# A hardware loop of two rounds around one wait on VectorE, ahead of the copy of the result

## Chip, cores, metric

One core of a Trainium2 chip. The metric is the device time of one execution in microseconds (us), and the profile is of one execution. PE is TensorE, DVE VectorE, ACT ScalarE, SP the engine that issues the transfers; "q" behind an engine's name means its sequencer, under which the profiles list branches (COMPARE_BRANCH), register arithmetic (ALU_OP, MOVE) and stand-alone waits (EVENT_SEMAPHORE).

## The reference

One token goes through a layer norm, an attention block over the last 4096 keys (32 query heads, 8 key heads) and a gated block of three matrices; the results are added to the token:

```python
x = A_x
xn = _layernorm(x, axis=-1)
return x + _A_ref(xn, A_k_cache, A_v_cache, A_wq, A_wo) + _B_ref(xn, B_w_r, B_w_gate, B_w_up, B_w_down)
```

With one row everything is a vector by a matrix, so the bytes to be loaded (30.7 MB) matter more than the arithmetic: in the profile before, DMA is 76% of the chain that ended last.

## The kernel before

All weights and caches come over one queue on SP. The last matrix, `B_w_down`, comes in four chunks of 7, 4, 2 and 1 rows per partition, each with its own semaphore:

```python
wd_chunks = [(0, 7), (7, 11), (11, 13), (13, 14)]
t_wd = [dma(sy, f"wd{k}", wd_sb[:, j0 * D:j1 * D], wd_v[:, j0 * D:j1 * D]) for k, (j0, j1) in enumerate(wd_chunks)]
# ... cut ...
    DVE.need(t_g4, t_rf)
    fill(2)
    t_part = DVE.mark(ve.tensor_tensor(out=part, in0=a_ps, in1=rf, op=ALU.add))      # L542
    PE.need(t_hT)
    for k, (j0, j1) in enumerate(wd_chunks):
        PE.need(t_wd[k])
        for j in range(j0, j1):
            ins = by_halves(hTr[:, j, 0:1], wd_sb[:, j * D:(j + 1) * D], stop=(j == FB - 1))   # L528
        if k == 0:
            PE.need(t_part, t_sel4)
            by_halves(sel4[:], part)
    t_a = PE.mark(ins)
    DVE.need(t_a)
    ACT.need(t_a)
    t_r0 = DVE.mark(ve.tensor_copy(out=res[:, 0:HD], in_=g_ps[0]))                   # L554
    t_r1 = ACT.mark(ac.copy(out=res[:, HD:], in_=g_ps[1]))                           # L555
    SP.need(t_r0, t_r1)
    t_out = dma(sy, "out", out.rearrange("a b d -> (a b) d"), res)
```

`need` puts a semaphore wait on an engine and `mark` lets an instruction raise that engine's counter. PE multiplies the chunks as they land; when its last product is done, VectorE copies the left half of the result and ScalarE the right half; when both are done, SP sends the output.

## Time and profile before

| | before |
|---|---|
| time, median of 6 runs | 79.82 us (79.73 to 79.94) |
| span of the profile, granted TensorE clock | 77.8 us, 1.0 |
| share of DMA in the chain that ended last | 76% |
| third chunk releases PE / fourth chunk releases PE | 75.21 / 75.53 us |
| the two copies start | 75.84 us |
| output issued | 76.30 us |

The chain is read backwards from the last instruction: at each step, what released it. Here it is transfers until 73.3, then PE on the four chunks, then VectorE's copy and the output. The lines that carry this stand in the prediction.

### The profile page before, as it was taken

To read this page: it belongs to the slowest core of one execution; us is meant where nothing else is said; L and a number is where in the kernel's file an instruction comes from. 1 tells how busy PE (TensorE), PEld (TensorE's weight loads), DVE (VectorE), ACT (ScalarE), POOL (GpSimd) and SP (SyncE) were. 2 spreads that over 40 slices of the span, in tenths; PEclk is the share of its full clock that TensorE was granted. 3 is DMA by queue.
4 is the path that set the end of the run, shared out by engine and by line. 5 is a ranking of instruction groups with operands and counts; after the bars stand their busy time and mean duration, and the time that the engine had idled before them with its cause. 6 is when DMAs were issued, how large, how long until landed. Compare 5 with 4: busy or idle time off the path is not lost.

```text
span 77.8 us, 1639 instructions
## 1 busy us (share of the span) xinstructions
PE 55.1 (71%) x640; PEld 28.9 (37%) x642; DVE 43.6 (56%) x96; ACT 30.3 (39%) x41; POOL 10.2 (13%) x22
## 2 busy tenths in 40 slices
PE   0010596479939979979976866877878891998890
PEld 0010311267618658658652342222223440342330
DVE  2779300389049797696945438898886357000301
ACT  2760102328945895895681070443333320000001
POOL 3950000003101032022049100000000000000000
DMA  6999999999999999999999999999999999999800
GB/s 135 387 405 413 438 425 421 425 446 430 472 438 404 413 421 455 446 421 404 408 438 446 446 396 421 412 446 427 413 457 405 430 455 438 404 396 401 319 29 1
DMA packets 2745, 30.72 MB, mean 395 GB/s; under 512 B 307, under 2 KB 438, under 8 KB 822
## 3 DMA queue, kind: packets, MB, share of 16 engines
q1 hardware_dynamic: 2738, 30.67, 93.8%
q8 instruction: 2, 0.03, 0.2%
q14 instruction: 1, 0.01, 0.0%
q10 hardware_dynamic: 4, 0.00, 0.0%
HBM read 30.67 MB, written 0.00 MB: 394 GB/s over the span
## 4 chain that ended last, share of the span: by engine, by line
DMA 76%; PE 9%; ACT 4%; DVE 3%; SPq 3%; issue 1%
DMA k_sb<-in_B_w_down_dram 52%; DMA k_sb<-in_A_k_cache_dram 25%; PE ps L354 5%; ACT kT L329 4%; PE ps L528 3%; SPq L189 3%; DVE kin L321 2%; PE ps L363 1%; DVE kT L326 1%; DVE kT L554 1%; SPq L84 0%; SPq L95 0%
## 5 line engine op out<-in xcount | busy, mean ns | idle before, releaser
L329 ACT COPY kT<-ps 128x1024 bf16<-128x1024 bf16 x19 | 18.5, 1016 | 8.3 <-PE ps L354 8.3
L354 PE MATMUL ps<-perm_bf,kin 128*128 128x128 bf16 x256 | 17.1, 220 | 2.4 <-DVE kin L321 2.1
L354 PEld LDWEIGHTS ps<-perm_bf,kin 128*128 128x128 bf16 x256 | 14.3, 98 | 6.4 <-issue 3.6
L321 DVE COPY kin<-k_sb 128x2048 bf16<-128x2048 bf16 x16 | 10.9, 686 | 4.4 <-DMA k_sb<-in_A_k_cache_dram 3.6
L326 DVE COPY kT<-ps 128x1024 bf16<-128x1024 bf16 x13 | 9.0, 689 | 2.2 <-PE ps L354 1.8
L449 ACT CAST pvS<-ps 128x512 bf16<-128x512 f32 x8 | 4.7, 586 | 10.0 <-PE ps L455 10.0
L363 PE MATMUL ps<-kT,qAB 128*32 128x512 bf16 x68 | 6.8, 389 | 1.9 <-ACT kT L329 1.9
L185 PE MATMUL ps<-zmov,zst 128*128 128x512 bf16 x31 | 7.7, 380 | 0.2 <-issue 0.2
L314 POOL COPY qAB<-qpad 128x64 bf16<-128x64 bf16 x8 | 3.7, 462 | 30.8 <-PE ps L363 30.8
L429 DVE COPY vin<-v_sb 128x2048 bf16<-128x2048 bf16 x8 | 5.5, 686 | 1.1 <-PE ps L464 1.0
L435 DVE COPY vin<-v_sb 128x2048 bf16<-128x2048 bf16 x8 | 5.5, 684 | 0.0
L555 ACT CAST kT<-ps 1x256 bf16<-1x256 f32 x1 | 0.4, 363 | 12.9 <-PE ps L528 12.9
L464 PE MATMUL ps<-vin,pTcur 128*32 128x512 bf16 x32 | 3.2, 386 | 2.6 <-ACT pvS L449 2.2
L476 PE MATMUL ps<-zmov,zst 128*128 128x512 bf16 x16 | 4.7, 376 | 0.0
L542 DVE TENSOR_TENSOR kT<-ps,kT 128x512 f32<-128x512 f32 x1 | 0.7, 691 | 6.5 <-PE ps L523 6.5
L185 PEld LDWEIGHTS ps<-zmov,zst 128*128 128x128 bf16 x32 | 2.7, 98 | 3.7 <-issue 1.3
L238 PE MATMUL ps<-ident_bf,xn_row 1*128 1x1 bf16 x4 | 0.3, 166 | 5.2 <-DVE xn_row L233 5.2
L299 DVE COPY qpad<-ps 128x16 bf16<-128x16 bf16 x4 | 0.5, 170 | 5.5 <-PE ps L294 5.5
L523 PE MATMUL ps<-k_sb,oT 128*1 128x512 bf16 x32 | 2.1, 378 | 2.0 <-DMA k_sb<-in_A_wo_dram 2.0
L470 PE MATMUL ps<-vin,pTcur 128*32 128x512 bf16 x32 | 3.2, 387 | 0.3 <-DVE vin L435 0.2
L282 PE MATMUL ps<-wq_sb,xnT 128*1 128x512 bf16 x32 | 2.9, 499 | 0.6 <-DMA wq_sb<-in_A_wq_dram 0.6
L363 PEld LDWEIGHTS ps<-kT,qAB 128*32 128x32 bf16 x68 | 1.9, 92 | 3.9 <-DVE kT L326 1.1
(95 smaller groups left out, 52.6 us busy)
## 6 DMA issues: line engine op xcount, KB each, us to landing
v_sb<-in_A_v_cache_dram SPq DMA_DIRECT2D x4, 2048.0 KB, 39.1
k_sb<-in_A_k_cache_dram SPq DMA_DIRECT2D x3, 2048.0 KB, 23.7
wq_sb<-in_A_wq_dram SPq DMA_DIRECT2D x2, 2048.0 KB, 9.4
k_sb<-in_A_wo_dram SPq DMA_DIRECT2D x2, 2048.0 KB, 36.1
k_sb<-in_A_k_cache_dram SPq DMA_DIRECT2D x2, 1024.0 KB, 14.2
wq_sb<-in_B_w_gate_dram SPq DMA_DIRECT2D x1, 1792.0 KB, 43.4
wq_sb<-in_B_w_up_dram SPq DMA_DIRECT2D x1, 1792.0 KB, 47.3
k_sb<-in_B_w_down_dram SPq DMA_DIRECT2D x1, 896.0 KB, 40.1
```

The lines of the kernel that those rows point to most:

```text
L185: te.matmul(ps[:, 7, :], lhsT=zst[:], rhs=zmov[:], start=True, stop=True)
L314: gp.tensor_copy(out=qAB[:], in_=qpad[:, g]).then_inc(s_q, 1)
L321: ve.tensor_copy(out=kin[:, 2 * h:2 * h + 2, :], in_=k_sb[:, g, 2 * h:2 * h + 2, :]).then_inc(s_c[h], 1)
L326: ve.tensor_copy(out=kT[:, b, :], in_=tp[:, b, :]).then_inc(s_ev[b], 1)
L329: ac.copy(out=kT[:, b, :], in_=tp[:, b, :]).then_inc(s_ev[b], 1)
L354: ins = te.transpose(tp[:, b, k * P:(k + 1) * P], kin[:, b, k * P:(k + 1) * P], perm_bf[:])
L363: ins = te.matmul(sc[32 * cq:32 * cq + 32, e, :], lhsT=qAB[:, e, :], rhs=kT[:, b, :].rearrange("d (k h q) -> d h k q", h=2, q=PH)[:, e], s ...
L429: ve.tensor_copy(out=vin[:, 0].rearrange("p (q k) d -> p q (k d)", q=4), in_=v_in[:, :, 0:4 * DH]).then_inc(s_va, 1)
L435: ve.tensor_copy(out=vin[:, 1].rearrange("p (q k) d -> p q (k d)", q=4), in_=v_in[:, :, 4 * DH:]).then_inc(s_vb, 1)
L449: ac.copy(out=pvS[:].rearrange("p t d -> p (t d)"), in_=pv_ps).then_inc(s_pvs, 1)
L464: ins = te.matmul(pv_ps[32 * tl:32 * tl + 32, :], lhsT=pTcur[:, tl].rearrange("p q e r -> p (q e r)"), rhs=vin[:, 0].rearrange("p (q t) d ...
L476: te.matmul(ps[:, 7, :], lhsT=zst[:], rhs=zmov[:], start=True, stop=True)
```

## The change

The intent: VectorE is made to run a loop of two rounds, each with a wait for the third chunk, before its copy. In the profile before, the third chunk releases PE at 75.21 us and the copy starts at 75.84, so the wait is met before the copy could start, and what is added is the loop's own work.

```diff
     t_a = PE.mark(ins)
+    with ve.Fori(0, 2):
+        ve.wait_ge(*t_wd[2])
     DVE.need(t_a)
     ACT.need(t_a)
     t_r0 = DVE.mark(ve.tensor_copy(out=res[:, 0:HD], in_=g_ps[0]))
```

## The prediction

What no trace or run of this case shows is cut from the recorded texts, here and below, and the cuts are marked. The sum below came to 0.635 us; its term for the branch back is cut. The terms that stand come to 0.50 us; with the two figures for that branch that the prediction works out from the trace, 0.09 and 0.27, they give its low case of 0.59 and its high case of 0.77. The factor 1.25 in its terms is an estimate, from the semaphore instruction's 21 ns on VectorE against 17 on ScalarE (1.24): with 1.24 each of them rounds to the same hundredth.

> **What bounds the kernel now.** I read the page's slices first, then the chain that ended last in order of time, then the timeline of the last five microseconds, because the change touches only the last wait of VectorE.
>
> The slices and the chain say that the transfers set the pace until about 73 us:
>
> ```profile
> PE   0010596479939979979976866877878891998890
> DVE  2779300389049797696945438898886357000301
> DMA  6999999999999999999999999999999999999800
> ...
> DMA 76%; PE 9%; ACT 4%; DVE 3%; SPq 3%; issue 1%
> ```
>
> The DMA row stands at 9 in nearly every slice, and DMA is 76% of the chain; VectorE (DVE) is almost idle in the last six slices. The end of the chain in order of time:
>
> ```profile
> 33.21 40.08 DMA k_sb<-in_B_w_down_dram
> 73.29 0.14 issue
> 73.43 2.39 PE ps L528 x32
> 75.82 0.02 issue
> 75.84 0.41 DVE kT L554
> ```
>
> The first chunk of A_w_down lands at 73.29, TensorE (PE) then works through the four chunks until 75.82, and VectorE's copy of the result is the last computing step. So a delay of that copy's start moves the end one for one. The timeline of the tail shows how much room there is:
>
> ```profile
> 75.21 0.09 PEld L528 LDWEIGHTS ps<-k_sb,hTr 128*1 128x1 bf16 x4 [0.28 <-DMA k_sb<-in_B_w_down_dram]
> 75.53 0.08 PEld L528 LDWEIGHTS ps<-k_sb,hTr 128*1 128x1 bf16 x2 [0.23 <-DMA k_sb<-in_B_w_down_dram]
> 75.84 0.36 ACT L555 CAST kT<-ps 1x256 bf16<-1x256 f32 x1 [12.86 <-PE ps L528]
> 75.84 0.41 DVE L554 CAST kT<-ps 1x256 bf16<-1x256 f32 x1 [2.92 <-PE ps L528]
> 76.30 0.32 SPq L189 DMA_DIRECT2D out_dram<-kT  x1
> ```
>
> The x4 row is the third chunk (two rows of weights, two halves each): PE was released by its landing at 75.21. The x2 row is the fourth chunk, at 75.53. The two copies start together at 75.84, ScalarE's ends at 76.20, VectorE's at 76.25, and the output is issued at 76.30. The new wait is on the third chunk, so VectorE can leave its first round at about 75.21 and has to be ready for its copy at 75.84: **the slack is 0.63 us**.
>
> [...] The trace has such instructions, and they differ by engine:
>
> ```profile
> L84 ACTq COMPARE_BRANCH  x1: 33/33/33, 1.1 to 1.1; - x1
> ...
> L84 DVEq COMPARE_BRANCH  x1: 47/47/47, 1.1 to 1.1; - x1
> ...
> L84 PEldq COMPARE_BRANCH  x1: 174/174/174, 1.1 to 1.1; - x1
> ```
>
> That is the branch from the first block to the kernel: 33 ns on ScalarE, 47 on VectorE, 174 on TensorE. [...] The 47 against 33 ns (1.42), and the semaphore instruction's 21 ns on VectorE against 17 on ScalarE (1.24), agree that VectorE's sequencer is slower. TensorE's loops show what one round consists of:
>
> ```profile
> L537 PEldq ALU_OP  x8: 36/36/36, 66.5 to 69.3; - x8
> L537 PEldq COMPARE_BRANCH  x8: 83/215/215, 66.6 to 69.4; - x8
> L537 PEldq MOVE  x1: 35/35/35, 66.4 to 66.4; - x1
> ```
>
> One MOVE sets the counter, each round has one ALU_OP and one COMPARE_BRANCH; a branch taken back is 215 ns and the last, not taken, is 83.
>
> [...] the copy before the change began 0.02 us after PE's last matmul ended. [...]
>
> [...] The page's queues show three fetches by the program:
>
> ```profile
> q8 instruction: 2, 0.03, 0.2%
> q14 instruction: 1, 0.01, 0.0%
> ```
>
> **The change part by part.** Nothing is removed. On VectorE the order of instructions gets an ALU_OP that carries the wait for the third chunk and a COMPARE_BRANCH, run twice, after the addition on L542 and ahead of the copy, plus a MOVE ahead of the loop. TensorE gets one unconditional branch after its last matmul, which releases nothing. Transfers and matmuls stay in order.
>
> - MOVE: runs when the addition of L542 has been dispatched, no later than about 72.9, over two microseconds before the wait ends. Cost on the path 0.
> - Two ALU_OP: 36 ns on PE, times 1.25 for the slower sequencer, 45 ns each: 0.09 us (estimate).
> - Branch taken: PE's 215 less its plain branch of 174 leaves 41 for the comparison; with VectorE's own 47 that would be 0.09 us. PE's 215 times 1.25 would be 0.27. [...]
> - Branch not taken: PE's 83 times 1.25 is 0.10 us.
> - Gaps between sequencer instructions: in the trace's single records of PE's loops the COMPARE_BRANCH begins 97 to 102 ns after its ALU_OP began, so the gap is about 61 to 66 ns; times 1.25 about 0.08. There are three: 0.24 us.
> - From the last sequencer instruction to the copy: on VectorE a semaphore wait of 21 ns began at 49.75 and the copy after it at 49.81. I take 0.07 us.
>
> Sum: 0.09 + [...]0.10 + 0.24 + 0.07 = **0.635 us**, against a slack of 0.63. So the loop ends about when PE does. With the low branch it is 0.59 (hidden by 0.04), with the high one 0.77 (a delay of 0.14). As a check, a whole round of PE's loop with four PE instructions in it takes (69.3 - 66.5) / 7 = 0.40 us, and its last half round (36 + 63 + 83) 0.18; together with 0.07 that is 0.65 us, the same. The share of the first round that lies before the wake is nil, since the first ALU_OP itself waits.
>
> The copy itself keeps its 0.41 us, and ScalarE's copy is not delayed, but the output waits for both. Mean expected delay 0.05 to 0.1 us, on 79.82: **79.9 us**, 0.1% up.
>
> **The rivals.**
> 1. *Fully hidden.* Sequencer work of VectorE is cheaper than I make it (47 ns for a plain branch speaks for it). Time 79.8, within the spread of the runs before (79.75 to 79.89).
> 2. *The loop breaks the fetch of instructions.* If the branch back dropped what was already fetched[...], the sequencer would fetch after 75.3. A transfer of 1 KB, the output's, lands about 1.1 us after its issue instruction in the trace, and the fetch packets themselves took 0.3 to 1.0 us; so 1 to 2 us, less nothing, as the slack is spent: 80.9 to 81.9, and the upper end is over 2%. Against it: none of the TensorE loops shows it (the first branch back of L371 took 223 ns, the later ones 207 to 215)[...]. I give it 5%.
> 3. *The tail moves for another reason.* A fetch of 16 KB[...] began at 74.3 in the trace, among the last transfers; a change in layout could move it and with it the last landings, by a few tenths either way. [...] A gain from it would stay under 0.5 us.
> 4. *VectorE waits longer because it sees the third chunk late.* The same semaphore released PE at 75.21; nothing suggests that VectorE sees it later.
>
> **Range and chances.** The centre is 79.9. From below the time is held by the transfers, unchanged, less a few hundredths of noise: 79.7. From above, the high branch (0.14), the spread of the runs (0.07) and some unknown cost of the loop's start (0.1 to 0.2) give 80.25. Two per cent is 1.6 us; only a fetch or a cost three times my estimate would reach it: 4%. Faster by 2% would need shorter transfers, which nothing touches: 1%.
>
> **What would show it right or wrong.** In the changed profile VectorE should have one MOVE, two ALU_OP and two COMPARE_BRANCH of the new line 552, the first ALU_OP at about 75.2 and the last branch over by about 75.8. The gap from PE's last matmul to VectorE's copy, 0.02 us before, should be 0 to 0.2; ScalarE's copy should keep its place behind PE. A branch on VectorE of over 0.3 us, or a new packet of kind "instruction" near 75 us, would show the second rival. Landings that moved relative to the span's start would show the third. A copy that starts a microsecond or more after PE's last matmul would make the prediction wrong.

## The result

| | before | after |
|---|---|---|
| time, median of 6 runs each | 79.82 us (79.73 to 79.94) | 79.77 us (79.66 to 79.78) |
| ratio | | 0.9989 (95%: 0.9976 to 1.0002) |
| span, clock of the profile | 77.8 us, 1.0 | 77.8 us, 1.0 |

The times are the same.

The new line 552 in the profile after, by its instructions (count, duration in ns as least/median/most, first and last start in us):

```profile
L552 DVEq ALU_OP  x2: 40/46/52, 75.2 to 75.5; - x2
L552 DVEq COMPARE_BRANCH  x2: 50/62/73, 75.3 to 75.6; - x2
L552 DVEq MOVE  x1: 44/44/44, 72.2 to 72.2; - x1
```

The MOVE ran at 72.2, while the addition of L542 was being executed; the first ALU_OP waited until 75.2, when the third chunk landed; the last branch began at 75.6. The tail of the timeline after:

```profile
75.21 0.09 PEld L528 LDWEIGHTS ps<-k_sb,hTr 128*1 128x1 bf16 x4 [0.27 <-DMA k_sb<-in_B_w_down_dram]
75.53 0.08 PEld L528 LDWEIGHTS ps<-k_sb,hTr 128*1 128x1 bf16 x2 [0.23 <-DMA k_sb<-in_B_w_down_dram]
75.85 0.36 ACT L557 CAST kT<-ps 1x256 bf16<-1x256 f32 x1 [13.09 <-PE ps L528]
75.85 0.41 DVE L556 CAST kT<-ps 1x256 bf16<-1x256 f32 x1 [2.94 <-PE ps L528]
```

The rows have not moved, and VectorE's copy still starts with ScalarE's, which has no loop in front of it. That is the test to use in all that follows: **ScalarE's copy marks the moment at which PE's end lets a copy begin; the distance of VectorE's copy from it is what the loop costs.** Here it is 0.00.

In the trace's single records the loop reads: ALU_OP 75.199 (52 ns), branch back 75.290 (73 ns), ALU_OP 75.516 (40 ns), branch not taken 75.592 (50 ns), over at 75.642. In the experiments below, where the loop ends late, the copy began 0.045 to 0.046 us after that, so here it was ready at 75.69 (an estimate: 75.642 + 0.046) and waited 0.16 us more for PE.

### The profile page after: what moved, and what is told of

Read it like the earlier page. It is cut to its first block, busy times and chain, and to the rows that moved or that the text cites. A ratio compares the mean times of both kernels' runs of the same rounds, so it can differ in the third digit from the quotient of the medians.

```text
span 77.8 us, 1644 instructions
## 1 busy us (share of the span) xinstructions
PE 56.0 (72%) x640; PEld 29.0 (37%) x642; DVE 43.5 (56%) x96; ACT 30.4 (39%) x41; POOL 10.1 (13%) x22
## 4 chain that ended last, share of the span: by engine, by line
DMA 76%; PE 9%; ACT 4%; DVE 3%; SPq 3%; issue 1%
DMA k_sb<-in_B_w_down_dram 52%; DMA k_sb<-in_A_k_cache_dram 25%; PE ps L354 5%; ACT kT L329 4%; PE ps L528 3%; SPq L189 3%; DVE kin L321 2%; PE ps L363 1%; DVE kT L326 1%; DVE kT L556 1%; SPq L84 0%; SPq L95 0%
## 5 line engine op out<-in xcount | busy, mean ns | idle before, releaser
L542 DVE TENSOR_TENSOR kT<-ps,kT 128x512 f32<-128x512 f32 x1 | 0.7, 691 | 6.7 <-PE ps L523 6.7
L282 PE MATMUL ps<-wq_sb,xnT 128*1 128x512 bf16 x32 | 3.8, 621 | 0.4 <-DMA wq_sb<-in_A_wq_dram 0.4
```

The lines of the kernel that those rows point to most:

```text
L282: ins = te.matmul(ps[32 * c:32 * c + 1, hf, :], lhsT=xnT[:, kt:kt + 1], rhs=wq_sb[:, kt, (4 * hf + c) * 512:(4 * hf + c + 1) * 512], start ...
```

## The experiments

**Theory:** the loop costs VectorE's sequencer about 0.49 us, from the landing of the third chunk to a copy that could start, and 0.65 us lie between that landing and the copy's start anyway. **Rivals:** A, a loop costs once and its rounds next to nothing; B, the end is set elsewhere, whatever VectorE does; C, such work costs the end wherever it lies; D, a wait for a landing is what costs or saves (the expectation of run 4 uses this letter for another one, that two rounds cost nearly nothing); and the fetch rival of the prediction. All runs gave the reference's result. Each ran beside the kernel before on the same chip. In runs 1 to 9 some executions, of the kernel before too, came at 80.5 to 80.9 us with a mean granted clock of 0.978 (others at that clock came at the usual time; runs 8 and 9 show what one of them was); they widen the intervals to some half or whole per cent. So hundredths of a microsecond are read from profiles only, against the same profile's ScalarE copy, and times are used for the larger effects. Eight of the twelve profiles below have a granted clock of 1.0; where it was lower, the text says so.

### 1 and 2: four rounds, eight rounds

```diff
-    with ve.Fori(0, 2):
+    with ve.Fori(0, 4):        # and 8 in the second run
         ve.wait_ge(*t_wd[2])
```

> Four rounds instead of two, same wait for the third chunk. Theory (sequencer work hidden behind the fourth chunk and PE's tail, 0.317 us a round as in the changed trace, 0.13 for the last half round, some 0.05 to the copy): the loop wakes at 75.20 and the copy can start at 75.20 + 3 x 0.317 + 0.13 + 0.05 = 76.33 instead of 75.85, so +0.48 us, 80.25 us. Rival A (a loop costs a fixed amount once, the rounds are nearly free): at most +0.1 us, 79.9. Rival B (the loop is hidden whatever its length, since the end is set elsewhere, by the landing of the output or the drain): 79.8.

> Eight rounds, same wait. Theory: copy at 75.20 + 7 x 0.317 + 0.13 + 0.05 = 77.60, so +1.75 us, 81.5 us, slope 0.317 us a round against the run with four rounds. Rival A (fixed cost): 79.9. Rival B (end set elsewhere): 79.8. If the branch back has to fetch instructions again, a round costs a microsecond or more and it would be over 85 us.

Four rounds: 80.16 us (79.99 to 80.36), before 79.83, ratio 1.0036 (0.9986 to 1.0085). Eight rounds: 81.20 us (81.01 to 81.71), ratio 1.0165 (1.0108 to 1.0222). The times alone resolve only the second. VectorE's copy in the timeline of the run with four rounds, 0.39 us behind ScalarE's at 75.80:

```profile
76.19 0.41 DVE L556 CAST kT<-ps 1x256 bf16<-1x256 f32 x1 [3.35 <-PE ps L528]
```

With eight rounds (profile at clock 0.97) the chain itself runs through the loop. The columns are start, length, what; "issue" is time in which the engine waited for nothing that the profile shows:

```profile
75.44 0.15 issue
75.60 0.04 DVEq L552
75.64 0.04 issue
75.67 0.06 DVEq L552
...
77.44 0.41 DVE kT L556
```

ScalarE's copy began at 75.93, so the loop cost 1.51 us. One round is 0.04 + 0.04 + 0.06 + 0.15: addition, gap, branch, and 0.15 until the next round's first instruction (rounded; 0.278 in the records). Between four and eight rounds the loss grew by 1.51 - 0.39 = 1.12 us, 0.28 a round. Rivals A and B fall. Both losses are smaller than expected (0.48 and 1.75), mainly because I had taken 0.317 for every round, and only the first takes that (its addition 52 ns, its branch 73); the later ones take 0.28. No round shows a microsecond for a fetch.

### 3: eight rounds, begun at the first chunk

```diff
-    with ve.Fori(0, 2):
-        ve.wait_ge(*t_wd[2])
+    with ve.Fori(0, 8):
+        ve.wait_ge(*t_wd[0])
```

> Eight rounds as well, but the wait is for the first chunk of A_w_down, which lands 1.9 us earlier (73.3). Theory (what counts is when the loop can begin, not how long it is): loop over at 73.32 + 7 x 0.317 + 0.13 = 75.67, copy ready at about 75.72, before PE's end at 75.82, so 79.8 us, as before. Rival C (loop work of VectorE's sequencer costs the end its length, or slows semaphores or the queue, wherever it lies): about as the other run with eight rounds, 81.5 us.

79.84 us (79.77 to 80.6) against 79.83, ratio 1.0019 (0.9961 to 1.0078). The copies in the timeline:

```profile
75.86 0.36 ACT L557 CAST kT<-ps 1x256 bf16<-1x256 f32 x1 [11.20 <-PE ps L528]
75.86 0.41 DVE L556 CAST kT<-ps 1x256 bf16<-1x256 f32 x1 [2.96 <-PE ps L528]
```

The same eight rounds that cost 1.51 us now cost none, as they ran from 73.30 to 75.41. Rival C falls: the length of the loop does not count, only when it is over.

### 4: two rounds, begun at the fourth chunk

```diff
-        ve.wait_ge(*t_wd[2])
+        ve.wait_ge(*t_wd[3])
```

> Two rounds, but the wait is for the fourth and last chunk, which lands 0.32 us after the third. Theory: first ALU_OP at about 75.51, last branch over at 75.51 + 0.317 + 0.13 = 75.96, copy at about 76.01 instead of 75.85, so +0.15 to +0.18 us, 79.95 us: the slack left by the change (0.15 us) is less than the 0.32 between the chunks. Rival B (end set elsewhere) and rival D (the change is harmless because two rounds cost nearly nothing): 79.8 us, copy still within 0.03 us of PE's end.

79.97 us (79.81 to 80.18), ratio 1.0007 (0.9969 to 1.0045): the times do not resolve it. The profile does. ScalarE's copy began at 75.88, VectorE's here:

```profile
76.04 0.41 DVE L556 CAST kT<-ps 1x256 bf16<-1x256 f32 x1 [3.10 <-PE ps L528]
```

That is 0.16 us late, within the 0.15 to 0.18 expected. Two rounds do cost; with the third chunk they fit in, with the fourth, 0.32 us later, they do not.

### 5: the wait without a loop

```diff
-    with ve.Fori(0, 2):
-        ve.wait_ge(*t_wd[2])
+    ve.wait_ge(*t_wd[2])
```

> The wait for the third chunk alone, without a loop, ahead of VectorE's copy. Theory: it is over at 75.20, and the copy needs 0.05 us after it, so it starts with PE's end as before, 79.8 us; the copy begins within 0.03 us of PE's last matmul's end, and the output is issued at 76.30. Rival D (what keeps the change harmless is that the loop replaces a wait that was costly): this run would differ from 79.8.

79.97 us (79.72 to 80.87) against 79.95. The profile missed the expectation of 0.03 us; the end of the chain:

```profile
75.82 0.03 issue
75.85 0.02 DVEq L34
75.87 0.04 issue
75.91 0.41 DVE kT L555
```

The copy started 0.07 us behind ScalarE's (75.84), which the change's loop did not cause. With the plain wait the copy has two semaphores to wait for, and the build moved one to an instruction of the sequencer, the 21 ns on L34. It moved the wait for PE, the late one: PE was done at 75.82, the instruction on L34 ran at 75.85, and the copy began 0.04 us after its end. In the change the wait for the chunk sits on the loop's addition, the copy keeps a single wait, and it began 0.02 us after PE's end (75.83 and 75.85). That the place of the late wait makes the difference is a reading; run 12 tests it.

### 6: the loop with nothing to hide behind

```diff
-        ve.wait_ge(*t_wd[2])
+        ve.wait_ge(*t_a)
```

> The same loop of two rounds, but around the wait for PE's last matmul itself, so that nothing is left to hide it behind. Theory: the whole cost of the loop shows, first ALU_OP at about 75.83, then 0.317 + 0.126 + 0.046 = 0.49 us to the copy at 76.32 instead of 75.85: +0.47 us, 80.3 us. With the sum of my prediction (0.635 us) the copy would start at 76.46 and it would be 80.4. Rival B (end set elsewhere): 79.8.

80.22 us (80.12 to 80.92) against 79.95, ratio 1.0034 (0.9949 to 1.0119); here too only the profile resolves it. The end of the chain shows every term of the loop's price:

```profile
75.82 0.05 DVEq L552
75.87 0.04 issue
75.91 0.07 DVEq L552
75.98 0.15 issue
76.14 0.04 DVEq L552
76.18 0.04 issue
76.21 0.05 DVEq L552
76.26 0.04 issue
76.31 0.41 DVE kT L556
```

From 75.82 to 76.31 it is 0.49 us, the theory's figure and not the 0.635 of the prediction. Against ScalarE's copy (75.82) the loss is the same 0.49.

### 7: eight rounds on ScalarE

```diff
-    with ve.Fori(0, 2):
-        ve.wait_ge(*t_wd[2])
+    with ac.Fori(0, 8):
+        ac.wait_ge(*t_wd[2])
```

> Eight rounds on ScalarE ahead of its own copy, waiting for the third chunk; VectorE without a loop. Theory: rounds cost a sequencer's time, [...]so 0.22 us a round (VectorE's later rounds took 0.278) and 0.25 for the first; ScalarE's copy at about 75.20 + 0.25 + 6 x 0.22 + 0.1 + 0.05 = 76.9 and its end at 77.3, where VectorE's copy ends at 76.26; the output waits for both: +1.0 us, 80.8 us. If the round were set by something the engines share (semaphores, memory), 0.28 us as on VectorE and 81.2. If it is like PE's loop (0.4 us with its four instructions) 82.

81.21 us (81.16 to 81.41), ratio 1.0136 (1.0062 to 1.0210); profile at clock 0.97. VectorE's copy, now without a loop, began at 75.78, and ScalarE's here:

```profile
76.88 0.36 ACT L557 CAST kT<-ps 1x256 bf16<-1x256 f32 x1 [13.65 <-issue]
```

ScalarE's later rounds took 0.228 us in the trace's records (addition to addition), VectorE's 0.278: a ratio of 1.22, near the 1.24 of the semaphore instruction (21 against 17 ns in the profile before). The expected 0.22 a round (an estimate, 0.278 over 1.24) held, so a round is the sequencer's own time. The time of 81.21 is the figure that the expectation gave to its rival, a limit that the engines share (81.2), but it doesn't speak for it: by the ratio it is 1.1 us above the kernel before, and ScalarE's copy began 1.10 us behind VectorE's, where the theory said about 1.0 and rounds of 0.28 would have made it 1.4.

### 8 and 9: a probe of the fetch that failed

The prediction gave 5% to a loop that makes the sequencer fetch instructions. The expectations of runs 8 to 11 take a border of two pages of instructions to lie at slot 256; that was an assumption when they were written, and what run 10 shows there is a step: 0.15 to 0.16 us from one no-operation to the next, against 0.03. To force this border into a loop, I put one into VectorE's idle time before L542 of the kernel before, with its first instruction placed by the build at a chosen slot:

```diff
+    with ve.bass.Fori(0, 3, engines=[mybir.EngineType.DVE], head_slot={mybir.EngineType.DVE: 236}):   # 190 in the control
+        for _ in range(22):
+            ve.nop(nofuse=True)
     DVE.need(t_g4, t_rf)
```

> A probe of the rival that a branch back makes the sequencer fetch instructions. Not the change: the kernel before, with a loop of three rounds of 22 no-operations in VectorE's idle time between 65.7 and 72.2 us, whose head is put at slot 236 of 256 so that its body lies across the border of two pages of instructions. If the two pages stay resident: a branch back costs some 0.25 us as in the change, a round 22 x 0.06 to 0.09 + 0.3 = 1.6 to 2.3 us, no packets of kind instruction other than at the entry, and the loop is over by about 73. If the branch back drops the first page: a gap of 1 to 3 us behind each branch taken, with packets of kind instruction beside it, loop over at 75 to 78, and since the addition of L542 comes after it, the time goes up by 2 to 5 us, to 82 to 85.

> The control of the run with the loop across two pages: the same loop with its head at slot 190, so that it ends at 214 and lies in one page. A branch back costs some 0.2 to 0.25 us, a round 1.6 to 2.3 us, no packets of kind instruction beside it. The loop is over by 71 to 73 us; the addition of L542 is ready at 72.2, so the time is 79.8, or up to 0.8 us more if a no-operation takes 0.09 us.

79.85 us (79.71 to 80.83) and 80.22 us (79.57 to 80.67), against 79.95. The traces show why nothing can be read from them: the 22 no-operations are missing, the build had dropped them, so a round was an addition and a branch (slots 236 and 237, by counting) and slot 256 did not lie in it. The 0.06 to 0.09 us that the two expectations give a no-operation were an estimate that run 10 does not bear out (0.03).

The profile of the control is one of the long executions (80.67 us, clock 0.978) and shows what made it long. The rows of the granted clock, in tenths for 40 slices of the span, in this profile and in that of run 12, which has the same mean clock and came at 79.73 us:

```profile
PEclk9999999999999999999999999999999999569999
PEclk9999999965999999999999999999999999999999
```

In the control the clock was 0.5 from 66.7 to 70.2, where TensorE had no idle time; VectorE's addition began at 73.74 instead of 72.22, and the copies 0.9 us later than in run 8. In run 12, and in runs 2 and 7 as far as the copies, the low stretch lay between 16 and 20 us, and the copy without a loop ahead of it stayed at 75.8 to 75.9. So these profiles put the longer time down to where the low stretch falls, and not to the mean clock. That the other long executions were of this kind is not shown, as none of them was profiled.

### 10 and 11: the probe with instructions that stay

```diff
-            ve.nop(nofuse=True)
+            ve.engine_nop()
```

> The probe of the fetch rival again, since the first attempt lost its no-operations in the build (three rounds of an empty loop, at slot 236 and 190). Now 22 no-operations of the engine's kind, which stay, so that the body runs from slot 236 across the border at 256 and back, three rounds, in VectorE's idle time before the addition of L542. If both pages stay resident: from a branch to the next round 0.13 to 0.16 us as before, packets of kind instruction at the entry to the second page at most, loop over by 71, time 79.8. If each branch back across the border fetches: one packet of kind instruction or more for each of the two branches taken, a gap of 1 to 3 us each, loop over by 70 to 75, time 79.8 to 83.

> Control: the same loop of 22 no-operations at slot 190, within one page. A gap of 0.13 to 0.16 us behind each branch taken, no packet of kind instruction near it, rounds of equal length, time 79.8.

Across the border 80.08 us (80.01 to 80.11) against 79.82 (79.62 to 80.26), ratio 1.0026 (0.9986 to 1.0066); in one page 79.76 us, a single run. The two branches back across the border, and the two of the control:

```profile
L540 DVEq COMPARE_BRANCH  x2: 62/64/67, 68.1 to 69.3; - x2
L540 DVEq COMPARE_BRANCH  x2: 63/63/63, 65.9 to 66.8; - x2
```

In the trace's records a round took 1.13 to 1.16 us across the border and 0.89 inside a page (branch to branch). The gap from a branch taken to the next instruction was 0.25 to 0.29 us, where 0.13 to 0.16 had been expected, against 0.16. From the start of the 20th no-operation to that of the 21st, which is slot 256, it was 0.15 to 0.16 us against 0.03; at the first crossing it was 0.41. So crossing slot 256 cost some 0.1 to 0.14 us each way, and the branches back brought no packets of their own: there is one more packet of kind instruction, not one for each branch. Part 3 of the page, across the border:

```profile
q14 instruction: 2, 0.02, 0.1%
```

The kernels before and after and the control have one. The fetch rival as I put it, 1 to 2 us for a branch back, does not come true even for a loop that does cross slot 256 (0.25 to 0.29 us behind a branch). A branch over a longer distance was not tested.

The additional packet (8 KB, 0.33 us long) began at 71.15, when the loop was over (70.5), among the last transfers. The fourth chunk's row in the timelines, across the border and in the control:

```profile
75.95 0.08 PEld L528 LDWEIGHTS ps<-k_sb,hTr 128*1 128x1 bf16 x2 [0.23 <-DMA k_sb<-in_B_w_down_dram]
```

```profile
75.62 0.08 PEld L528 LDWEIGHTS ps<-k_sb,hTr 128*1 128x1 bf16 x2 [0.23 <-DMA k_sb<-in_B_w_down_dram]
```

It is 0.33 us later, as long as the packet: of the chunk's 16 parts, 14 landed as in the control, within 0.1 us, and the last two 0.70 and 0.32 us later. The profile of run 10 also ran 1.9 us behind the control before its loop began (VectorE's L514 at 66.74 against 64.85), but run 3's did so too (66.75) and its tail did not move. The late parts fit a fetch that holds up transfers behind it, and the four times of 80.01 to 80.11 fit too; but it is one profile of each, and the interval of the ratio includes 1, so it is likely and not shown.

### 12: the wait carried by a no-operation

```diff
     ve.wait_ge(*t_wd[2])
+    ve.engine_nop()
     DVE.need(t_a)
```

> The plain wait for the third chunk, but carried by a no-operation of the engine ahead of the copy. In the run with the plain wait the copy had two waits, the one for PE had become an instruction of the sequencer of its own, and the copy began at 75.91, 0.065 us after that instruction, not at 75.85. Theory (that instruction, not the wait for the third chunk, cost the 0.065): with the wait moved onto a no-operation the copy has only PE's wait,[...] and begins about 0.36 to 0.37 us after the fourth chunk's landing as in the kernel before, 75.84 to 75.86 where that landing is at 75.48. Rival (any wait on a landing here costs 0.06): 0.43 us after it, 75.91.

79.73 us, one look (clock 0.978). The copy in the timeline:

```profile
75.82 0.41 DVE L556 CAST kT<-ps 1x256 bf16<-1x256 f32 x1 [2.95 <-PE ps L528]
```

ScalarE's began at 75.82 too, and the fourth chunk had landed at 75.46, 0.36 us before. So the 0.07 us of run 5 came from where the late wait was put, not from the wait for the chunk, and rival D falls. It is no gain over the kernel before, which has no such wait to place, and no run here points to a kernel faster than both.

## Why the prediction was right

- **The mechanism held.** "The slack is 0.63 us" came out as 0.65 (75.20 to 75.85). The delay was forecast as 0 to 0.14 and was 0.00; 79.77 us lies in the range of 79.7 to 80.25, and the first rival, fully hidden, is what happened. Runs 3, 4 and 6 show that hiding, and not a free loop, is the reason: the same loop shows 0.16 or 0.49 us as soon as it starts later. The time alone would have shown little, as the range begins at no delay; a wrong price of the loop could have fallen into it too.
- **The loop's price was too high by 0.15 us.** Forecast 0.635 us, measured 0.49, so the loop was over 0.16 us before it was needed and not about when PE was, and the mean delay of 0.05 to 0.1 us did not come. By terms: the two additions 0.09 forecast, 0.092 measured. The branch back (the figures from the trace were 0.09 and 0.27) with the gap behind it (0.08 forecast): 0.073 + 0.153 measured, in sum within the 0.17 to 0.35 of those figures, but wrong in its parts. The branch not taken 0.10 forecast, 0.050 measured: TensorE's 83 ns times 1.25 was the wrong source; ScalarE's 40 ns (run 7), times 1.24, would have given it. The gaps from addition to branch 0.08 each forecast, 0.039 and 0.036 measured, again taken over from TensorE. From the last branch to the copy 0.07 forecast, 0.046 measured. ScalarE would have been the better source for the whole: in run 7 its first round took 0.245 us, and its last addition with what follows up to the copy 0.142; times 1.24 that is an estimate of 0.48 us.
- **The cross-check confirmed nothing.** It was built from the same TensorE loop.
- **"A branch back drops what was fetched"** (5%): not in the change, which has the same three packets of kind instruction as the kernel before, and not in run 10 either.
- **"The tail moves for another reason"**: it did not in the change, but run 10 makes the size of that rival plausible, some 0.3 us.
- **What the prediction did not see**: that the bare wait would have been slightly worse than the loop (run 5, 0.07 us in the profile).
- **Smaller slips in the working.** The unconditional branch on TensorE did not come: the trace after has five instructions more (1644 against 1639), all of them VectorE's of L552. The later branches back of L371 took 207 to 208 ns; 215 is that of other loops. That the loop holds back the copy behind it was not shown when the prediction was written; run 6 shows it, where PE was done at 75.79, before the loop began, and the copy began at 76.31, 0.045 us after the last branch.

## What to carry to other kernels

In these runs a loop on VectorE's sequencer cost only what it ended later than the PE result that the copy waited for anyway (0.00 us in the change and run 3, 0.16 to 1.51 in runs 1, 2, 4 and 6). To see that ahead of a run, find the moment the sequencer's work can begin, add its length, and compare it with the start of the next engine instruction. Here 2.1 us of loop cost nothing when begun at one landing and 1.5 us when begun at another. Where an engine instruction ends a chain, leave it with a single wait, the late one, and put earlier waits on an instruction ahead of it: the profiles of runs 5 and 12 show 0.07 us for it, too little for the times to resolve. And take a price for sequencer work from the same engine where the trace has one: here a forecast built mostly on TensorE's was 0.15 us too high.

The prices measured here: a compare-and-branch lasted 50 ns not taken and 56 to 73 taken on VectorE, 40 and 45 to 50 on ScalarE (run 7), 76 to 83 and 207 to 223 on TensorE (profile before); and after a taken one it was another 0.15 us on VectorE and 0.12 on ScalarE to the next round's first instruction. A short round, addition and branch, took 0.28 us on VectorE and 0.23 on ScalarE. From the sequencer's last instruction to the copy it was 0.045 to 0.046 us on VectorE (runs 1, 2, 4 and 6) and 0.042 on ScalarE (run 7). Crossing slot 256 cost VectorE's loop 0.1 to 0.14 us more each way (run 10). The packets on the queue that got one more there (q14) were of 8 KB, those on the other (q8) of 16 KB (8192 and 16384 bytes in the trace before).
